# Second mixture: the scaled combine weights are turned by VectorE blocks and DMAs instead of TensorE transposes

## The chip, the cores and the metric

The kernel runs on one core of one Trainium2 chip. The metric is the device time of one execution in microseconds (us). Before the change three runs took 1120.14, 1126.13 and 1126.85 us, median 1126.13 us. The execution that the profiler recorded took 1125.19 us; its span from the first to the last instruction is 1123.3 us, so 1.9 us lie around the span.

## The reference

Three stages follow each other: an attention block, a first mixture of experts with slots, and a second mixture whose weights are balanced. Only the last is touched by the change:

```python
def _moe_ref(x, phi, w1, w2):            # the first mixture
    ...
    c = exp(logits - logits.max(1)); c /= c.sum(1) + 1e-9     # (2304, 32)
    return c @ slot_out                                       # slot_out: (32, 512)

def _moe2_ref(x, w_gate, w1, w2):        # the second, N, D, E, F = 2304, 512, 8, 1024
    logits = x @ w_gate
    P = exp(logits - logits.max())
    for _ in range(8):                   # balance rows and columns
        P /= P.sum(1) + 1e-9
        P /= P.sum(0) + 1e-9
        P *= N / E
    for e in range(E):
        h = maximum(x @ w1[e], 0)
        out += P[:, e:e+1] * (h @ w2[e])
```

Since x = c @ slot_out, the kernel never forms x in the second mixture. It takes x @ w1[e] as c @ (slot_out @ w1[e]). P is positive, so P[:, e] is multiplied into c ahead of the maximum, and the products of an expert can be added up without a further factor. All products are made to nearly full float32 precision from a rounded part ("high", h) and a remainder ("low", l).

## The kernel before

The 2304 tokens are 18 tiles of 128. A **unit** is two token tiles (256 tokens) of one expert; an expert has nine units (NU = 9), eight experts have 72, and they run one after the other. Each unit has seven **steps** k = 0 to 6.

`c4T` holds the combine weights with 128 partitions: four blocks of 32 slots (high, high, low, low), along the tokens. `a4s[e]` holds slot_out @ w1[e] in the matching blocks. `layer1(g)` (L1118) multiplies both: 8 matmuls per unit give the hidden values of the unit. `layer1(g + 1)` is issued behind step 1 of unit g.

From unit 5 on a unit's second layer is a seven-product scheme (Strassen's kind): `product` (L1424 to L1426) issues 12 matmuls of 128x256 per step, so 84 per unit, from sums of hidden values s1 to s4, a11, a12, a22 (high and low) and sums of weights T1 to T4, BB1, BB2. `hidden` makes the hidden sums on VectorE (DVE, L1142, L1155), ScalarE (ACT, L1138, L1148) and GpSimd (POOL, L1159); `collect` adds the products into accA, accB and accD on DVE (L1440).

Beside this, each expert e from 1 on needs, ahead of its own units:

- `load_w1`, `load_raw`: eight loads of 512 KB on the queue of SyncE (SP), L984 and L977.
- `prepare_a` (L1065): 32 small matmuls in unit 1 of expert e - 1 into the PSUM tile pa; `split_a` (L1074, L1076), and `move_a` (L1098): 16 DMAs of 32 KB into `a4s[e]`.
- the weight sums and their high and low parts: `w_sum`, `w_hi`, `w_lo` (L1018, L1021, L1027), mostly on POOL.
- its scaled combine weights in `c4T`. This is what the change replaces. Five times per expert (`c_steps`), for units 0-1, 2-3, 4-5, 6-7 and 8, in units 6, 7 and 8 of expert e - 1 and in units 0 and 1 of expert e itself: `scale_c` multiplies c by P on DVE (L1289), rounds on ACT (L1294), writes the high part twice on ACT (L1298) and the remainder twice on DVE (L1299); `turn_c` (L1304) transposes four tiles of 128x128 on TensorE (PE) into the PSUM tile pc, two tiles the fifth time; `store_c` (L1309) copies pc to `c4T` on ACT.

PE, DVE, ACT and POOL run in the order in which the program is written (a manual schedule): `beside(s, f)` puts a helper at step s = 7 * unit + k behind that step's product. Each engine works through its own list and waits at the first instruction whose inputs are not there. The SP queue issues its DMAs in the order that the planner gives it, one after the other. Each DMA uses one of eight semaphores in turn, so it waits for the one that was issued eight places earlier.

Of the kernel before, what the change touches and what calls it, by code (L numbers as in the profile page):

```python
# [8 lines left out]
F32 = mybir.dt.float32  # L9
BF16 = mybir.dt.bfloat16  # L10
F32R = mybir.dt.float32r
# [10 lines left out]
def infini_attention_soft_moe_sinkhorn_moe(  # L22
# [1002 lines left out]
    def w_lo(e, nm, i, g):  # L1025
# [9 lines left out]
    Cw = mD.tile([P, NTT, NS], F32, name="Cw")  # L1035
    sel = mD.tile([P, 4, 160], F32R, name="sel")
    nc.vector.tensor_scalar(
        out=sel.rearrange("p j c -> p (j c)"), in0=ones[:, 0:1].to_broadcast([P, 640]),
        scalar1=0.0, scalar2=None, op0=ALU.mult,
# [19 lines left out]
    def prepare_a(e):  # L1059

        w1 = w1s.pop(e)
        pa = aux("pa")
        for c in range(KD):
            for j in range(4):
                nc.tensor.matmul(  # L1065
                    pa[32 * j : 32 * j + 32, 0:256], soT[:, c, :], w1[j][:, c, :],
                    start=(c == 0), stop=(c == KD - 1),
                )
        a2s[e] = pa

# [126 lines left out]
    m2 = mS.tile([1, 1], F32, name="m2")  # L1197

    def gate_slots():
        soB = G["soB"] = mB.tile([P, KD, 4, NS], F32, tag="c4", name="soB")  # L1200
        nc.scalar.activation(out=soB, in_=soR.to_broadcast([P, KD, 4, NS]), func=AF.Copy)
# [84 lines left out]
    def scale_c(e, u0, u1):  # L1286
        T0, n = 2 * u0, 2 * (u1 - u0)
        cP = mB.tile([P, 4, NS], F32, tag="cP", name="cP")[:, 0:n]
        nc.vector.tensor_tensor(  # L1289
            out=cP, in0=Cw[:, T0 : T0 + n], in1=Pr[:, T0 : T0 + n, e : e + 1].to_broadcast([P, n, NS]),  # L1290
            op=ALU.mult,
        )
        chi = mB.tile([P, 4, NS], F32R, tag="chi", name="chi")[:, 0:n]
        nc.scalar.activation(out=chi, in_=cP, func=AF.Copy)  # L1294
        c4 = cs_[e, u0] = mB.tile([P, 4, 4, NS], F32, tag="c4", name="c4")
        hb = chi.bitcast(F32).rearrange("p t (o s) -> p t o s", o=1).to_broadcast([P, n, 2, NS])
        cb = cP.rearrange("p t (o s) -> p t o s", o=1).to_broadcast([P, n, 2, NS])
        nc.scalar.activation(out=c4[:, 0:n, 0:2, :], in_=hb, func=AF.Copy)  # L1298
        nc.vector.tensor_tensor(out=c4[:, 0:n, 2:4, :], in0=cb, in1=hb, op=ALU.subtract)  # L1299

    def turn_c(e, u0, u1):
        pc = G["pc"] = aux("pc")
        for t in range(2 * (u1 - u0)):
# [4 lines left out]
    def store_c(e, u0, u1):  # L1308
        nc.scalar.activation(  # L1309
            out=c4T[:, UT * u0 : UT * u1], in_=G["pc"][:, 0 : UT * (u1 - u0)], func=AF.Copy  # L1310
        )


    side = {}
# [27 lines left out]

    def c_steps(v, e, u0, u1):
        at(v, 1, scale_c, e, u0, u1)
        at(v, 2, turn_c, e, u0, u1)
        at(v, 3, store_c, e, u0, u1)

    for k, u0, u1 in ((-1, 5, 7), (2, 7, 9)):
        for n, f in enumerate((scale_c, turn_c, store_c)):
            at(RAW - 1, k + n, f, 0, u0, u1)  # L1350
    s = 1
    for i in range(2):
# [9 lines left out]
    for e in range(1, E):  # L1362
        v = NU * (e - 1)
        for i in range(5):
            c_steps(v + 6 + i, e, 2 * i, min(2 * i + 2, NU))
        at(v, 0, load_w1, e, e % 2)
# [3 lines left out]
        at(v + 1, 4 + (e == 1), split_a, e)  # L1370
        at(v + 1, 5 + (e == 1), move_a, e)
        for i in range(2):
# [41 lines left out]
    def product(g, k):  # L1414
# [7 lines left out]
        wh, wl = W[e, b, "h"], W[e, b, "l"]  # L1422
        for f in range(KH):
            nc.tensor.matmul(o_, hh[:, f, :], wh[:, f, :], start=f == 0, stop=False)  # L1424
            nc.tensor.matmul(o_, hh[:, f, :], wl[:, f, :], start=False, stop=False)  # L1425
            nc.tensor.matmul(o_, hl[:, f, :], wh[:, f, :], start=False, stop=f == KH - 1)  # L1426
        return o_
# [197 lines left out]
```

## Time and profile before

| | |
|---|---|
| median of three runs | 1126.13 us |
| the profiled execution | 1125.19 us, span 1123.3 us |
| granted TensorE clock, mean over the span | 0.988 |
| second mixture, seven-product units | about 387 us to the end |
| issues of `a` by `move_a` | 112 in all, 32 KB each |

The page's first part gives busy time by engine, its second part the same in 40 slices of 28 us each with the granted clock. A matmul's row lasts 0.28 us, but the next one starts 0.11 us later, since they are pipelined; so the distance between starts, not the length of a row, tells what a matmul costs. In the chain of waits "PE l L1118 x8" is a unit's `layer1`; from one such row to the next is exactly one unit's work on PE.

### The profile page before, as it was taken

To read this page: it belongs to the slowest core of one execution; us is meant where nothing else is said; L and a number is where in the kernel's file an instruction comes from. 1 tells how busy PE (TensorE), PEld (TensorE's weight loads), DVE (VectorE), ACT (ScalarE), POOL (GpSimd) and SP (SyncE) were. 2 spreads that over 40 slices of the span, in tenths; PEclk is the share of its full clock that TensorE was granted. 3 is DMA by queue.
4 is the path that set the end of the run, shared out by engine and by line. 5 is a ranking of instruction groups with operands and counts; after the bars stand their busy time and mean duration, and the time that the engine had idled before them with its cause. 6 is when DMAs were issued, how large, how long until landed. Compare 5 with 4: busy or idle time off the path is not lost.

```text
span 1123.3 us, 24568 instructions
## 1 busy us (share of the span) xinstructions
PE 1080.5 (96%) x9269; PEld 988.4 (88%) x9269; DVE 832.4 (74%) x1813; ACT 644.3 (57%) x1392; POOL 703.7 (63%) x634
## 2 busy tenths in 40 slices
PE   6999898988999999999999999999999999999998
PEld 4777777764477899999999999999999999999998
DVE  7777777764167467788778878877877787788876
ACT  7988888751242666456545645654564464556442
POOL 5755545410153587678678767867776786778665
PEclk9999999997989999999999999999999999999999
DMA  7677875348912003003200400220040022000111
GB/s 178 200 218 228 239 248 136 86 152 363 370 56 75 1 5 147 20 1 113 58 1 2 150 21 1 99 71 3 1 151 20 1 95 73 5 2 6 53 57 57
DMA packets 42647, 105.73 MB, mean 94 GB/s; under 512 B 8225, under 2 KB 18593, under 8 KB 38433
## 3 DMA queue, kind: packets, MB, share of 16 engines
q1 hardware_dynamic: 42096, 104.07, 28.5%
q8 instruction: 74, 1.21, 0.4%
q14 instruction: 45, 0.36, 0.1%
q10 hardware_dynamic: 432, 0.09, 0.0%
HBM read 95.74 MB, written 4.72 MB: 89 GB/s over the span
## 4 chain that ended last, share of the span: by engine, by line
PE 83%; DVE 5%; issue 4%; DMA 4%; ACT 3%; POOL 1%; SPq 0%; DVEq 0%; ACTq 0%; POOLq 0%
PE y L1424 19%; PE y L1425 19%; PE y L1426 19%; PE l L1118 6%; PE po L455 4%; PE pt L418 2%; PE y L1391 2%; DMA wm<-in_moe_w_dram 2%; PE pa L1065 1%; PE pc L1304 1%; PE ps L373 1%; ACT sm L379 1%; DMA w<-in_moe_w_dram 1%; PE ps L374 1%; PE ps L359 1%
## 5 line engine op out<-in xcount | busy, mean ns | idle before, releaser
L1142 DVE SCALAR_TENSOR_TENSOR f<-l,f 128x512 f32<-128x512 f32 x268 | 184.1, 687 | 61.2 <-ACT a11h L1148 53.6
L1159 POOL TENSOR_TENSOR s1l<-f,s1h 128x512 fp32r<-128x512 f32 x67 | 90.2, 1347 | 153.6 <-ACT s1h L1148 153.6
L1440 DVE TENSOR_TENSOR accA<-accA,y 128x512 f32<-128x512 f32 x125 | 85.5, 684 | 42.8 <-PE y L1426 42.3
L1148 ACT ACTIVATE a12h<-l 128x512 fp32r<-128x512 f32 x72 | 43.2, 601 | 97.1 <-PE y L1426 91.4
L1159 POOL TENSOR_TENSOR s4l<-f,s4h 128x512 fp32r<-128x512 f32 x67 | 87.4, 1304 | 15.7 <-PE y L1425 13.0
L1440 DVE TENSOR_TENSOR accB<-accB,y 128x512 f32<-128x512 f32 x125 | 85.6, 685 | 5.6
L1159 POOL TENSOR_TENSOR s3l<-f,s3h 128x512 fp32r<-128x512 f32 x67 | 87.2, 1301 | 0.0
L1159 POOL TENSOR_TENSOR s2l<-f,s2h 128x512 fp32r<-128x512 f32 x67 | 87.0, 1298 | 0.0
L1118 PE MATMUL l<-c4T,a 128*128 128x256 f32 x576 | 80.3, 283 | 2.3 <-DVE a22l L1155 2.3
L1138 ACT ACTIVATE f<-l 128x512 f32<-128x512 f32 x67 | 39.7, 592 | 74.3 <-PE l L1118 73.2
L1027 POOL TENSOR_TENSOR BB1l<-raw,BB1h 128x512 fp32r<-128x512 f32 x32 | 41.4, 1305 | 61.7 <-ACT BB1h L1021 61.7
L1424 PE MATMUL y<-T2h,s2h 128*128 128x256 f32 x268 | 77.5, 289 | 0.0
L1118 PEld LDWEIGHTS l<-c4T,a 128*128 128x128 f32 x576 | 73.2, 192 | 4.2 <-DVE a22l L1155 3.8
L1424 PE MATMUL y<-BB2h,a12h 128*128 128x256 f32 x268 | 74.9, 279 | 0.0
L1425 PE MATMUL y<-BB2l,s4h 128*128 128x256 f32 x268 | 74.7, 279 | 0.0
L1424 PE MATMUL y<-BB1h,s3h 128*128 128x256 f32 x268 | 74.6, 278 | 0.0
L1426 PE MATMUL y<-BB1h,s3l 128*128 128x256 f32 x268 | 74.5, 278 | 0.0
L1425 PE MATMUL y<-BB1l,s3h 128*128 128x256 f32 x268 | 74.5, 278 | 0.0
L379 ACT ACTIVATE sm<-sm,mn 128x128 f32<-128x128 f32 (+3 forms) x128 | 70.8, 554 | 6.5 <-DVE mn L375 6.2
L1425 PE MATMUL y<-T2l,s2h 128*128 128x256 f32 x268 | 74.5, 278 | 0.0
L1426 PE MATMUL y<-T2h,s2l 128*128 128x256 f32 x268 | 74.4, 278 | 0.0
L1424 PE MATMUL y<-BB2h,s4h 128*128 128x256 f32 x268 | 74.3, 277 | 0.0
(315 smaller groups left out, 4203.9 us busy)
## 6 DMA issues: line engine op xcount, KB each, us to landing
wm<-in_moe_w_dram SPq DMA_DIRECT2D x32, 1024.0 KB, 8.2
raw<-in_moe_w_dram SPq DMA_DIRECT2D x32, 512.0 KB, 4.1
w<-in_moe_w_dram SPq DMA_DIRECT2D x32, 512.0 KB, 4.3
qd<-in_q_dram SPq DMA_DIRECT2D x30, 288.0 KB, 4.4
kd<-in_k_dram SPq DMA_DIRECT2D x30, 288.0 KB, 4.6
qp<-in_q_dram SPq DMA_DIRECT2D x15, 288.0 KB, 3.8
vt<-in_v_dram SPq DMA_DIRECT2D x16, 256.0 KB, 2.8
out_dram<-accB SPq DMA_DIRECT2D x18, 128.0 KB, 1.8
```

Of the source, the lines that this page charges most:

```text
L379: nc.scalar.activation(out=sm[:, 0:n], in_=sm[:, 0:n], func=AF.Exp, scale=-1.0, bias=mnc, accum_out=X.sums[:, i, h : h + 1],)
L455: nc.tensor.matmul(po[64 * h : 64 * h + 64, c0:w], X.vt[:, j, h, :], rhs, start=(j == 0), stop=(j == n - 1),)
L1027: eng(g).tensor_tensor(out=w_tile(e, nm, "l")[:, h], in0=full(e, nm, i), in1=w_tile(e, nm, "h")[:, h].bitcast(F32), op=ALU.subtract,)
L1118: nc.tensor.matmul(ph[:, f, :], a4s[e][:, P * (KH * j + f) : P * (KH * j + f) + P], c4T[:, UT * u : UT * u + UT], start=True, stop=True,)
L1138: nc.scalar.activation(out=f_tile(g, nm), in_=ph(g, nm), func=AF.Relu)
L1142: nc.vector.scalar_tensor_tensor(out=f_tile(g, nm), in0=ph(g, src), scalar=0.0, in1=b, op0=ALU.max, op1=op)
L1148: nc.scalar.activation(out=h_tile(g, nm, "h"), in_=ph(g, nm) if a else FU[g, nm], func=AF.Relu if a else AF.Copy)
L1159: nc.gpsimd.tensor_tensor(out=lo, in0=FU[g, nm], in1=hi, op=ALU.subtract)
L1424: nc.tensor.matmul(o_, hh[:, f, :], wh[:, f, :], start=f == 0, stop=False)
L1425: nc.tensor.matmul(o_, hh[:, f, :], wl[:, f, :], start=False, stop=False)
L1426: nc.tensor.matmul(o_, hl[:, f, :], wh[:, f, :], start=False, stop=f == KH - 1)
L1440: nc.vector.tensor_tensor(out=acc, in0=acc, in1=y, op=ALU.add)
```

## The change

For experts 1 to 7, 16 of the 18 token tiles are turned without PE, in two rounds of eight tiles (r = 0: units 0 to 3, r = 1: units 4 to 7):

- `part_c` multiplies c by P on POOL (128x256), `round_c` rounds it on ACT, `rest_c` takes the remainder on POOL.
- `blocks_c` transposes 32x32 blocks with one DVE instruction of 128x256 for the high and one for the low part.
- `move_c` puts the blocks into place: 16 DMAs of 32 KB per round on the SP queue, each of 32 partitions by 8 runs of 128 bytes.

Round 0 stands in units 4 and 5 of expert e - 1 (one unit later for e = 1), round 1 in unit 1 of expert e, steps 0 to 4. The two tiles left over (unit 8) are still scaled by `scale_c` and transposed by PE, now straight ahead of the 32 matmuls of the next `prepare_a`, into the unused half of the same PSUM tile; `store_c` follows at step 5. `move_a` goes from unit 1 to unit 3. In unit 0 of an expert, the products with B and T3 weights issue the four matmuls that use a low weight part last. The tile `sel` is shared with the blocks, and small tiles are laid into shared ones.

```diff
     def prepare_a(e):
         w1 = w1s.pop(e)
-        pa = aux("pa")
+        pa = a2s[e] = aux("pa")
+        if e > 1:
+            turn_c(e - 1, NU - 1, NU)
...
     def turn_c(e, u0, u1):
-        pc = G["pc"] = aux("pc")
+        pc = G["pc"] = a2s[e + 1][:, 256:] if 0 < e < E - 1 else aux("pc")
...
+    NR = 8
+    WR = NR * NS
+    ct_ = {}
+
+    def part_c(e, r):
+        cw = ct_[e, r] = cw_tile()
+        nc.gpsimd.tensor_tensor(
+            out=cw[:, 0:WR].rearrange("p (t s) -> p t s", s=NS), in0=Cw[:, NR * r : NR * r + NR],
+            in1=Pr[:, NR * r : NR * r + NR, e : e + 1].to_broadcast([P, NR, NS]), op=ALU.mult,
+        )
+
+    def round_c(e, r):
+        cw = ct_[e, r]
+        nc.scalar.activation(
+            out=cw[:, WR : 2 * WR].bitcast(F32R), in_=cw[:, 0:WR], func=AF.Copy
+        )
+
+    def rest_c(e, r):
+        cw = ct_[e, r]
+        nc.gpsimd.tensor_tensor(
+            out=cw[:, 0:WR], in0=cw[:, 0:WR], in1=cw[:, WR : 2 * WR], op=ALU.subtract
+        )
+
+    def blocks_c(e, r, z):
+        if z == 0:
+            ct_[e, r, "t"] = mD.tile([P, 640], F32, tag="sel", name="ct")
+        cw = ct_[e, r]
+        nc.vector.transpose(
+            ct_[e, r, "t"][:, WR * z : WR * z + WR], cw[:, WR * (1 - z) : WR * (2 - z)]
+        )
+
+    def move_c(e, r, zs):
+        ct = ct_[e, r, "t"]
+        to = c4T[:, 0:N].bitcast(F32).rearrange("p (t j n) -> p t j n", j=4, n=32)
+        for z in zs:
+            for j in range(4):
+                nc.sync.dma_start(
+                    to[32 * z : 32 * z + 32, NR * r : NR * r + NR, j],
+                    ct[32 * j : 32 * j + 32, WR * (z // 2) : WR * (z // 2) + WR].rearrange(
+                        "p (t n) -> p t n", n=32
+                    ),
+                )
...
-    def c_steps(v, e, u0, u1):
-        at(v, 1, scale_c, e, u0, u1)
-        at(v, 2, turn_c, e, u0, u1)
-        at(v, 3, store_c, e, u0, u1)
+    def c_round(s, e, r):
+        for k, f, *a in (
+            (0, part_c), (1, round_c), (2, blocks_c, 0), (5, rest_c), (6, blocks_c, 1),
+        ):
+            beside(s + k, f, e, r, *a)
+        beside(s + 3, move_c, e, r, (0, 1))
+        beside(s + 7, move_c, e, r, (2, 3))
...
+    at(NU * (E - 1) + 1, 3, turn_c, E - 1, NU - 1, NU)
...
         v = NU * (e - 1)
-        for i in range(5):
-            c_steps(v + 6 + i, e, 2 * i, min(2 * i + 2, NU))
+        c_round(7 * (v + 4 + (e == 1)) + 2, e, 0)
+        for k, f, *a in (
+            (0, part_c), (1, round_c), (2, blocks_c, 0), (2, rest_c), (3, blocks_c, 1),
+            (3, move_c, (0, 1)), (4, move_c, (2, 3)),
+        ):
+            at(v + 10, k, f, e, 1, *a)
+        at(v + 10, 1, scale_c, e, NU - 1, NU)
+        at(v + 10, 5, store_c, e, NU - 1, NU)
...
-        at(v + 1, 5 + (e == 1), move_a, e)
+        at(v + 3, 3 * (e == 1), move_a, e)
...
+        terms = ((hh, wh), (hh, wl), (hl, wh))
+        seq = [(f, t) for f in range(KH) for t in terms]
+        if u == 0 and e and (b[0] == "B" or b == "T3"):
+            seq = [(f, t) for f in range(KH) for t in terms[::2]] + [(f, terms[1]) for f in range(KH)]
+        for n, (f, (a, b)) in enumerate(seq):
+            nc.tensor.matmul(o_, a[:, f, :], b[:, f, :], start=n == 0, stop=n == 3 * KH - 1)
```

Three places of the order show the move. First PE in unit 1 of expert 2, around the third and fourth step, before (y are the products' PSUM tiles, w the tiles of w1, c the scaled weights; the number is a buffer's):

```order
L1425 MATMUL y_7287<-BB1l,s3h 128x256
L1426 MATMUL y_7287<-BB1h,s3l 128x256
L1304 MATMUL pc<-ident,c_7284 128x128 x2
L1424 MATMUL y_7310<-T2h,s2h 128x256
L1425 MATMUL y_7310<-T2l,s2h 128x256
...
L1426 MATMUL y_7310<-T2h,s2l 128x256
L1065 MATMUL pa<-w_0_7079,soT 32x256
L1065 MATMUL pa<-w_1_7081,soT 32x256
```

and with the change:

```order
L1492 MATMUL y_7269<-T2l,s2h 128x256
L1492 MATMUL y_7269<-T2h,s2l 128x256
L1315 MATMUL pa<-ident,cf 128x128 x2
L1068 MATMUL pa<-w_0_7050,soT 32x256
L1068 MATMUL pa<-w_1_7052,soT 32x256
```

The two transposes that are left stand directly ahead of `prepare_a`; the four turns of four transposes, such as "L1304 ... x4" in each of the four units before, have no row any more. On PE there are 112 rows fewer in all.

Second, DVE in the same unit, before:

```order
L1440 TENSOR_TENSOR accB<-accB,y_7236 128x512
L1289 TENSOR_TENSOR cP<-Cw,Pr 128x64
L1299 TENSOR_TENSOR c_7284<-cP,chi 128x2x64
L1440 TENSOR_TENSOR accA<-accA,y_7256 128x512
L1142 SCALAR_TENSOR_TENSOR f<-l_7274,f 128x512 x2
L1440 TENSOR_TENSOR accD<-accD,y_7287 128x256
L1142 SCALAR_TENSOR_TENSOR f<-l_7269,f 128x512
```

and with the change:

```order
L1506 TENSOR_TENSOR accB<-accB,y_7194 128x512
L1300 TENSOR_TENSOR cf<-Cw,Pr 128x64
L1310 TENSOR_TENSOR cf<-cf 128x2x64
L1506 TENSOR_TENSOR accA<-accA,y_7216 128x512
L1144 SCALAR_TENSOR_TENSOR f<-l_7234,f 128x512
L1352 STREAM_TRANSPOSE ct<-cw 128x256
L1144 SCALAR_TENSOR_TENSOR f<-l_7234,f 128x512
L1506 TENSOR_TENSOR accD<-accD,y_7246 128x256
L1352 STREAM_TRANSPOSE ct<-cw 128x256
L1144 SCALAR_TENSOR_TENSOR f<-l_7229,f 128x512
```

The two block transposes of round 1 stand between the hidden sums of this unit. The second needs `rest_c`, which POOL makes.

Third, the SP queue from the raw loads for expert 2 to the first w1 load for expert 3, before:

```order
L977 DMA raw_5733<-in_moe_w_dram 128x1024
L977 DMA raw_5735<-in_moe_w_dram 128x1024
L977 DMA raw_5737<-in_moe_w_dram 128x1024
L977 DMA raw_5739<-in_moe_w_dram 128x1024
L1098 DMA a_5918<-ahi 32x256 x4
L1098 DMA a_5918<-alo 32x256 x4
L1098 DMA a_5918<-ahi 32x256 x4
L1098 DMA a_5918<-alo 32x256 x4
L984 DMA w_1_7081<-in_moe_w_dram 128x1024
```

and with the change:

```order
L977 DMA raw_5700<-in_moe_w_dram 128x1024
L977 DMA raw_5702<-in_moe_w_dram 128x1024
L977 DMA raw_5704<-in_moe_w_dram 128x1024
L977 DMA raw_5706<-in_moe_w_dram 128x1024
L1361 DMA c4T<-ct 32x8x32 x16
L1100 DMA a_5904<-ahi 32x256 x4
L1100 DMA a_5904<-alo 32x256 x4
L1100 DMA a_5904<-ahi 32x256 x4
L1100 DMA a_5904<-alo 32x256 x4
L1361 DMA c4T<-ct 32x8x32 x16
L984 DMA w_1_7052<-in_moe_w_dram 128x1024
```

Round 1 of expert 1 (16 DMAs) now stands behind the raw loads and ahead of `move_a`, and round 0 of expert 2 behind `move_a`, ahead of the next loads.

## Rows read from the trace of the kernel before

**Rows 1.** The page, first and second part: busy time by engine, then the granted clock in 40 slices.

```profile
PE 1080.5 (96%) x9269; PEld 988.4 (88%) x9269; DVE 832.4 (74%) x1813; ACT 644.3 (57%) x1392; POOL 703.7 (63%) x634
...
PEclk9999999997989999999999999999999999999999
```

**Rows 2.** Windows: two units without transposes and one with four.

```profile
core 0: us, PE busy (x) PEld busy (x) DVE busy (x) ACT busy (x) POOL busy (x), PEclk, DMA share, GB/s
655.14:665.57 10.43, 10.43 (x95) 10.43 (x94) 7.99 (x13) 5.17 (x9) 7.26 (x6) 1.00 0.10 24
952.30:963.14 10.84, 10.84 (x95) 10.84 (x94) 7.97 (x13) 5.11 (x9) 7.57 (x6) 1.00 0.10 23
498.84:510.03 11.19, 11.19 (x98) 11.19 (x98) 10.01 (x16) 6.10 (x12) 8.96 (x8) 1.00 0.01 2
```

**Rows 3.** Chain of waits in order of time: start us, us, what.

```profile
399.05 0.91 PE l L1118 x8
...
457.13 0.91 PE l L1118 x8
...
556.25 0.91 PE l L1118 x8
...
597.96 0.91 PE l L1118 x8
608.85 0.91 PE l L1118 x8
...
642.08 1.18 PE l L1118 x8
655.14 0.91 PE l L1118 x8
665.57 0.91 PE l L1118 x8
...
952.30 0.94 PE l L1118 x8
963.14 0.94 PE l L1118 x8
...
1050.74 0.91 PE l L1118 x8
```

**Rows 4.** Timeline of PE: start us, us, instruction; the distance of starts is the pitch.

```profile
500.60 0.28 PE L1424 MATMUL y<-BB1h,s3h 128*128 128x256 f32 x1
500.71 0.28 PE L1425 MATMUL y<-BB1l,s3h 128*128 128x256 f32 x1
...
734.95 0.28 PE L1424 MATMUL y<-BB2h,s4h 128*128 128x256 f32 x1
735.14 0.38 PE L1425 MATMUL y<-BB2l,s4h 128*128 128x256 f32 x1
```

**Rows 5.** DMA issues: KB each, median us to landing; then SP's timeline.

```profile
a<-ahi SPq DMA_DIRECT2D x56, 32.0 KB, 1.8
mbd<-in_M_prev_dram SPq DMA_DIRECT2D x8, 65.0 KB, 3.7
...
648.60 2.41 SPq L1098 DMA_DIRECT2D a<-ahi  x4
```

**Rows 6.** Groups by line and shape from 450 us on: busy us, mean ns of one, idle.

```profile
L1299 DVE TENSOR_TENSOR c<-cP,chi 128x256 f32<-128x256 f32 x24 | 20.9, 870 | 10.1 <-ACT chi L1294 10.1
L1440 DVE TENSOR_TENSOR accD<-accD,y 128x256 f32<-128x256 f32 x120 | 49.9, 415 | 2.9 <-PE y L1426 1.3
L1338 POOL TENSOR_TENSOR accD<-accD,accA 128x256 f32<-128x256 f32 x9 | 7.2, 797 | 4.9 <-DVE accA L1440 4.9
```

**Rows 7.** Timelines of POOL and DVE in unit 1 of expert 3.

```profile
640.45 1.29 POOL L1159 TENSOR_TENSOR s4l<-f,s4h 128x512 fp32r<-128x512 f32 x1
645.93 1.29 POOL L1159 TENSOR_TENSOR s1l<-f,s1h 128x512 fp32r<-128x512 f32 x1 [4.19 <-ACT s1h L1148]
...
644.50 1.49 DVE L1142 SCALAR_TENSOR_TENSOR f<-l,f 128x512 f32<-128x512 f32 x2 [0.50 <-ACT a11h L1148]
```

More of the change, by code (lines that the diff above doesn't have):

```diff
@@ L1035, in infini_attention_soft_moe_sinkhorn_moe @@
     Cw = mD.tile([P, NTT, NS], F32, name="Cw")
-    sel = mD.tile([P, 4, 160], F32R, name="sel")
+    sel0 = mD.tile([P, 640], F32, tag="sel", name="sel").bitcast(F32R)
+    sel = sel0.rearrange("p (j c) -> p j c", j=4)
     nc.vector.tensor_scalar(
-        out=sel.rearrange("p j c -> p (j c)"), in0=ones[:, 0:1].to_broadcast([P, 640]),
+        out=sel0, in0=ones[:, 0:1].to_broadcast([P, 640]),
         scalar1=0.0, scalar2=None, op0=ALU.mult,
@@ L1068, in prepare_a @@
                 )
-        a2s[e] = pa
     def split_a(e):
@@ L1197, in infini_attention_soft_moe_sinkhorn_moe, with cw_tile @@
     m2 = mS.tile([1, 1], F32, name="m2")
+    def cw_tile():
+        return mB.tile([P, 768], F32, tag="cw", name="cw")
     def gate_slots():
-        soB = G["soB"] = mB.tile([P, KD, 4, NS], F32, tag="c4", name="soB")
+        soB = G["soB"] = cw_tile()[:, 0:512].rearrange("p (c a s) -> p c a s", c=KD, a=4)
         nc.scalar.activation(out=soB, in_=soR.to_broadcast([P, KD, 4, NS]), func=AF.Copy)
@@ L1287, in scale_c @@
         T0, n = 2 * u0, 2 * (u1 - u0)
-        cP = mB.tile([P, 4, NS], F32, tag="cP", name="cP")[:, 0:n]
+        if e:
+            cw = mB.tile([P, 2, CW], F32, tag="ft", name="cf").rearrange("p a c -> p (a c)")
+        else:
+            cw = cw_tile()
+        o_ = 4 * NS * (2 if e else 4)
+        w = n * NS
+        cP = cw[:, o_ : o_ + w].rearrange("p (t s) -> p t s", s=NS)
         nc.vector.tensor_tensor(
@@ L1292, in scale_c @@
         )
[L1293 to L1296, printed above, removed]
+        chi = cw[:, o_ + w : o_ + 2 * w].rearrange("p (t s) -> p t s", s=NS)
+        nc.scalar.activation(out=chi.bitcast(F32R), in_=cP, func=AF.Copy)
+        c4 = cs_[e, u0] = cw[:, 0:o_].rearrange("p (t a s) -> p t a s", a=4, s=NS)
+        hb = chi.rearrange("p t (o s) -> p t o s", o=1).to_broadcast([P, n, 2, NS])
         cb = cP.rearrange("p t (o s) -> p t o s", o=1).to_broadcast([P, n, 2, NS])
@@ L1422, in product @@
         wh, wl = W[e, b, "h"], W[e, b, "l"]
[L1423 to L1426, printed above, removed]
+        terms = ((hh, wh), (hh, wl), (hl, wh))
[4 more added lines that the diff above has]
+            nc.tensor.matmul(o_, a[:, f, :], b[:, f, :], start=n == 0, stop=n == 3 * KH - 1)
         return o_
```

## The prediction

> **What bounds the kernel now.** I read the page first: PE is busy for 96% of the span, and from the sixteenth slice on the granted clock reads 9, the highest digit, in every slice [rows 1], and 1.00 in the windows of the second mixture [rows 2]: its upper level, 2.4 GHz. So the clock is no lever here. Next come the windows of the second mixture: in each unit PE is busy for the whole of it, DVE for 8.0 to 10.0 us, POOL for 7.3 to 9.0 us, ACT for 5 to 6 us [rows 2]. PE alone sets the end there. What an edit is worth is the PE time it takes out, plus the stalls of PE that it ends, less those that it makes. The chain of waits gives the currency: the distance between two `layer1` rows is one unit on PE. A unit without anything beside its 92 matmuls takes 10.43 us (655.14 to 665.57) [rows 3], or 0.113 us per matmul, the pitch that the timeline shows between two starts (500.60, 500.71) [rows 4].
>
> The same rows show something the busy shares hide. From 952.30 to 963.14 lies one unit with the same 92 matmuls, and it takes 10.84 us [rows 3], with PE just as full and the clock at 1.00 [rows 2]. Every matmul starts 0.118 us after the last, not 0.113. I call it the **slow pitch**. It persists from matmul to matmul; it lasted for four units here. It begins or ends only where the stream of products is interrupted: by transposes, by `prepare_a`, or by a stall. Such a stall is seen at 735.14, where a product waits for a low weight part, 0.19 us after the start before it in place of 0.11 [rows 4]. What starts it I can't say from the trace. So each interruption is a draw. By the pitch behind them, of the 28 four-transpose turns 6 were followed by it, as in the unit of 11.19 us [rows 2], and of the six `prepare_a` one, the one ahead of 952.30; a `layer1` row of 0.94 us in place of 0.91 marks it [rows 3].
>
> **The change, part by part.** *PE.* Seven experts lose four turns of four transposes, 112 in all. One such turn at the fast pitch makes a unit 10.89 us (597.96 to 608.85), so 0.46 us [rows 3], and 28 of them 12.9 us. But the turns also cost by what they leave behind, so I take whole experts. The unit that holds `prepare_a` and two transposes takes 13.06 us (642.08 to 655.14), of which 0.27 us is a wait in `layer1` (1.18 in place of 0.91) [rows 3]; so 12.79 us is what stays of it. An expert without other turns and at the fast pitch is then 8 x 10.43 + 12.79 = 96.23 us. Experts 2 to 6 ran from 457.13 to 952.30, five experts, 495.17 us; 5 x 96.23 is 481.15, so 14.0 us go. In expert 1, 399.05 to 457.13 is 58.08 us against 4 x 10.43 + 12.79 = 54.51: 3.6 us. The last expert, 952.30 to 1050.74, took 98.44 us; it has no `prepare_a`, and 8 x 10.43 + (10.43 + 0.23) = 94.10: 4.3 us. **Together 21.9 us**: 12.9 us of transposes, and 9.0 us of slow pitch and small stalls that come with them.
>
> *The slow pitch afterwards.* `prepare_a` remains, with the two transposes now in front of it, one interruption per expert, and 1 in 6 of these was followed by the slow pitch. With nothing behind it to end it, it would last the nine units to the next: 9 x 0.41 = 3.7 us. With a chance of 1 in 6 in each of seven experts, one such expert is the likeliest count (39%), none 28%, two 23%. I give back one: 3.7 us.
>
> *The DMAs.* 32 per expert come onto the SP queue, 224 in all. In the trace one DMA of `a` is issued every 0.6 us (four in 2.41 us), and lands after 1.8 us; mbd moves 64 partitions by 4 runs of 260 bytes, 256 runs as a move has, and lands after 3.7 us [rows 5]. A round of 16 thus takes 15 x 0.63 + 1.8 to 3.7, 11 to 13 us. Round 0 has over two units until `layer1` of the next expert. Round 1 is the tight one: the first block transpose stands behind the first hidden sum of unit 1, which starts at 644.50 in expert 3 [rows 7], so its DMAs start near 645.6; the first reader, `layer1` of unit 4, is two unit starts behind 642.08, at 665.57 [rows 3]. That leaves 20 us less the 0.27 us stall, 19.7 us, so 6 to 8 us of slack. I cost it at nothing; the cover is two units of products, and below is what it costs if it fails. `move_a`, pushed to unit 3 behind these, has until unit 8: nothing.
>
> *DVE.* Out go ten operations per expert, of which the 128x256 one alone takes 870 ns [rows 6]; in come four block transposes. The trace has no such operation. The nearest 128x256 rows give 415 ns (accD) and 870 ns (two inputs from SBUF) [rows 6]; a transpose has one input, as accD has one from SBUF, so I take 415. In unit 1 of an expert this is 8.0 us of the plain unit [rows 2] plus some 0.5 us for the two small operations plus 0.8 to 1.7 us: 10.2 us at the most, below 10.43, and near the 10.01 us that a four-turn unit already carried [rows 2]. Nothing.
>
> *POOL.* Four operations of 128x256 at 797 ns [rows 6], at most the 1.3 us of a 128x512 one [rows 7]. In unit 1 POOL is idle for 4.19 us ahead of s1l [rows 7], and both operations of round 1 go there. In units 4 and 5 one each, on 7.3 to 9.0 us [rows 2]. Nothing.
>
> *ACT* loses four copies of 128x512 and eight small activations per expert and gains two: nothing. *The reordered products* keep their twelve matmuls; they end stalls like that of 735.14, whose 0.08 us and slow pitch are in the 9.0 us already. Waiting for eight DMA semaphores is not new to `layer1`: unit 0 of each expert did so for `a`.
>
> **Sum**: 1125.2 - 21.9 + 3.7 = 1107.0 us. The profiled execution lies 0.9 us below the median of 1126.13, within the spread of the three runs.
>
> **Rivals.** *1. The slow pitch stays in most experts.* For it: in the last expert it held over four units [rows 3], and the turns that used to end it are gone. Against: five of six `prepare_a` ended it. Three to seven experts give 1103.3 + 3 x 3.7 to 7 x 3.7, 1114 to 1129 us, so no change. By the 1 in 6 alone it has 10%; as the new neighbour of `prepare_a` may change the draw for all, I say 15%.
>
> *2. Round 1 lands late, and the kernel is slower.* Place: `layer1` of unit 4 in seven experts. Each DMA waits for the one eight places earlier, so with a landing time L a round takes 15 x L / 8 + L once L is above 5 us. It is late from L = 6.9 us (2.88 x 6.9 = 19.7), takes the whole gain of 3.1 us per expert at L = 7.9 us, and at L = 10 us it is 9 us late, 63 us in all, 1170 us. For it: runs of 128 bytes in place of the 1024 of `a`, and no DMA of the trace moves so many. Against: the 3.7 us for as many runs of 260 bytes, out of HBM and with other loads in flight [rows 5]. 8%. The Trainium skill ("DMA: Bandwidth & Descriptors", Specifications) speaks for this rival: below 512 bytes a transfer is a read, a change and a write, and off line rate. If that doubled the 3.7 us to 7.4, the round would be 1.6 us late, and the sum 1118 us in place of 1107. By that rule mbd's 260-byte rows should pay it already; the trace has them at 3.7 us.
>
> *3. A new wait reaches PE.* DVE's second block transpose waits for POOL, which waits for ACT, which waits for POOL behind s4l; behind it on DVE stand s3 and the accumulations that free PSUM. By rows it is ready at 640.45 + 1.29 + 0.80 + 0.6 + 0.80 = 643.9, before DVE comes to it, and still with 1.3 us per POOL operation (644.9) [rows 7]. If 1 us per expert got through, 1114 us. 7%.
>
> **Chances.** Forecast with none to two experts at the slow pitch, 1103 to 1111 us: 70%. Rivals: 15, 8 and 7%. About 1%, 11 us, is what a measurement of this kernel can tell from no change. Faster by more (below 1115 us): all of the forecast, rival 3 mostly, a part of rival 1, 81%. Same: the rest of rivals 1 and 3 and the mild end of rival 2, 13%. Slower: rival 2 with L over 8.4 us, 6%. The range that leaves out 2 in 10 goes from 1101 (no slow pitch, and 2 us for the run) to 1116 us, with three experts at the slow pitch, or a new wait.
>
> **What would show it.** After: `layer1` rows 10.43 us apart in seven or eight units of each expert, and about 12.8 us where `prepare_a` stands. Slow pitch: 10.84 us in a row of units. Rival 2: `layer1` of unit 4 waiting for a DMA, and c4T landings of over 7 us. Rival 3: PE waiting for DVE in unit 1 or 5. The forecast is wrong if transposes that are gone leave units at 10.9 us, or the sum of the distances falls by less than 14 us.

## The result, and the profile after

The changed kernel took 1135.0 us in the median of 20 runs (1120.26 to 1142.43), the kernel before 1124.74 (1120.14 to 1131.56) beside it. The ratio is 1.0056, 95% interval 1.0037 to 1.0075: no faster, and if anything 0.6% slower. (The comparison leaves the longest runs out, so the ratio is nearer to 1 than the medians are; experiment e10 shows what one run of that length consists of.) The forecast was 1107.0 us.

The profiled run after took 1120.26 us, the shortest of the 20 and 14.7 us below their median; what is read from it holds for that run. First the page: busy time of PE and the granted clock, which answer to [rows 1], and the DMA issues (KB each, median us to landing), to [rows 5].

```profile
PE 1074.0 (96%) x9157; PEld 982.7 (88%) x9157; DVE 804.7 (72%) x1785; ACT 617.9 (55%) x1322; POOL 719.1 (64%) x662
...
PEclk9999999996999999999999999999999999999999
...
c4T<-ct SPq DMA_DIRECT2D x224, 32.0 KB, 2.0
```

The 112 transposes are gone (9269 instructions of PE to 9157), but PE's busy time fell by 6.5 us, not by the 12.9 that they cost. The new DMAs land after 2.0 us. Now groups by line from 380 us on: instruction, count, busy us, mean ns. They are the operations that [rows 6] were to stand in for.

```profile
L1352 DVE STREAM_TRANSPOSE ct<-cw 128x256 f32<-128x256 f32 x28 | 12.2, 436 | 3.0 <-POOL cw L1344 2.7
L1344 POOL TENSOR_TENSOR cw<-cw 128x256 f32<-128x256 f32 x14 | 10.4, 744 | 3.7 <-ACT cw L1338 3.7
L1331 POOL TENSOR_TENSOR cw<-Cw,Pr 128x256 f32<-128x256 f32 x14 | 9.1, 647 | 0.0
```

The chain of waits (start us, us, what) answers to [rows 3]; `layer1` is now L1120. The unit at 540.05, 636.92 and 736.86 is the one with `prepare_a`.

```profile
453.36 0.94 PE l L1120 x8
464.20 0.94 PE l L1120 x8
...
540.05 0.95 PE l L1120 x8
...
552.91 0.91 PE l L1120 x8
563.34 0.91 PE l L1120 x8
...
630.25 1.79 POOL BB2l L1027
...
636.92 1.19 PE l L1120 x8
...
650.17 0.94 PE l L1120 x8
...
736.86 0.97 PE l L1120 x8
...
749.74 0.91 PE l L1120 x8
...
946.58 0.91 PE l L1120 x8
...
1043.20 0.94 PE l L1120 x8
```

The units are what was forecast: 10.43 us at the fast pitch (552.91 to 563.34), 10.84 at the slow one (453.36 to 464.20), nothing at 10.9. But the pitch changes at every `prepare_a`: slow up to 540.05, then fast for one expert's length, then slow (650.17), and so on. Behind the last expert's two transposes, where no `prepare_a` stands, it is slow again (1043.20). And a POOL instruction, `BB2l`, stands on the path in unit 0 of the experts that run fast. The waits of PE's weight loads from 380 us on (us in all, times, longest) give its price:

```profile
PEld l L1120 <- DVE a22l L1157: 3.0, 5, 2.3
PEld y L1492 <- POOL BB2l L1027: 1.9, 4, 0.5
```

**Where the 13.3 us between 1107.0 and 1120.26 went**, against the 96.23 us of a fast expert. Three slow experts, 453.36 to 552.91 the first: 99.55, 99.57 and 99.57 us, 10.0 us over. Two fast ones, 552.91 to 650.17 the first, 97.26 us, 2.1 us over: 0.6 us each in unit 0, with the wait for POOL's `BB2l`, and 0.5 us each in the unit of `prepare_a` (636.92 to 650.17, 13.25 against 12.79), 0.28 of it the wait in `layer1` (1.19 in place of 0.91) that the forecast had taken off. The last one up to unit 65, 946.58 to 1043.20: 96.62 against 94.10, 2.5 us. Behind it five units at the slow pitch, 2.1 us, and the last 151 matmuls at 0.0045 us more each, 0.7 us. Together 17.4, less the 3.7 us that the forecast had given back: 13.7 us. Of the 0.4 us over, 0.2 are two further differences, the rest is rounding: `layer1` of 397.14 in this run came 1.9 us earlier than that of 399.05 before, and from there to 453.36 it took 56.2 us against the 54.51 of the forecast, 1.7 us more.

### The profile page after: what moved, and what is told of

It is laid out like the page before. It is cut to its first block, busy times and chain, and to the rows that moved or that the text cites. A ratio compares the mean times of both kernels' runs of the same rounds, so it can differ in the third digit from the quotient of the medians.

```text
span 1118.5 us, 24560 instructions
## 1 busy us (share of the span) xinstructions
PE 1074.0 (96%) x9157; PEld 982.7 (88%) x9157; DVE 804.7 (72%) x1785; ACT 617.9 (55%) x1322; POOL 719.1 (64%) x662
## 4 chain that ended last, share of the span: by engine, by line
PE 78%; issue 6%; POOL 5%; DVE 5%; ACT 3%; DMA 2%; SPq 0%; DVEq 0%; POOLq 0%; ACTq 0%
PE y L1492 55%; PE l L1120 5%; PE po L455 3%; PE pt L418 2%; POOL BB2l L1027 2%; PE ph L863 1%; DMA qp<-in_q_dram 1%; PE pso L885 1%; ACT sm L379 1%; PE pa L1068 1%; PE ps L373 1%; PE y L1455 1%; PE ps L374 1%; PE ps L359 1%; PE ps L354 1%
## 5 line engine op out<-in xcount | busy, mean ns | idle before, releaser
L1161 POOL TENSOR_TENSOR s1l<-f,s1h 128x512 fp32r<-128x512 f32 x67 | 87.1, 1300 | 128.7 <-ACT s1h L1150 116.6
L1120 PE MATMUL l<-c4T,a 128*128 128x256 f32 x576 | 79.2, 280 | 2.1 <-DVE a22l L1157 2.1
L1120 PEld LDWEIGHTS l<-c4T,a 128*128 128x128 f32 x576 | 72.3, 188 | 3.5 <-DVE a22l L1157 3.0
L1492 PE MATMUL y<-T2h,s2h 128*128 128x256 f32 x268 | 75.0, 280 | 0.0
L1492 PE MATMUL y<-T4h,a22h 128*128 128x256 f32 x268 | 74.7, 279 | 0.0
L1492 PE MATMUL y<-T4l,a22h 128*128 128x256 f32 x268 | 74.7, 279 | 0.0
L1492 PE MATMUL y<-T4h,a22l 128*128 128x256 f32 x268 | 74.7, 279 | 0.0
L1492 PE MATMUL y<-T1h,s1h 128*128 128x256 f32 x268 | 74.7, 279 | 0.0
L1492 PE MATMUL y<-T1l,s1h 128*128 128x256 f32 x268 | 74.7, 279 | 0.0
L1492 PE MATMUL y<-T1h,s1l 128*128 128x256 f32 x268 | 74.7, 279 | 0.0
```

Source lines behind the costliest of these rows:

```text
L1120: nc.tensor.matmul(ph[:, f, :], a4s[e][:, P * (KH * j + f) : P * (KH * j + f) + P], c4T[:, UT * u : UT * u + UT], start=True, stop=True,)
L1161: nc.gpsimd.tensor_tensor(out=lo, in0=FU[g, nm], in1=hi, op=ALU.subtract)
L1492: nc.tensor.matmul(o_, a[:, f, :], b[:, f, :], start=n == 0, stop=n == 3 * KH - 1)
```

## The experiments

Each experiment's runs stand beside runs of the kernel before on the same chip; ratios are to those. e1 to e4 share one such set, e5 to e8 a second, e9 to e11 a third, and e12 has a fourth, so times of different sets are compared by their ratios. Each profile is of one run.

**e1, the changed kernel again.** No edit.

> The changed kernel once more, for a second profile. Theory (the pitch of the products): the time follows the number of units that run at the slow pitch (10.84 us in place of 10.43), about 1105 us plus 0.41 us for each of up to 66 such units; a time of 1130 us or more shows the slow pitch in more than 50 units, and stalls of PE in the experts that sum to less than 5 us. Rival (late parts): the number of slow units stays near the 33 or so of the first profile, and what is longer is found in waits of PE for POOL, DVE or a DMA.

1124.8 us (1117.61 to 1128.74, 6 runs), ratio 0.9985 (0.9953 to 1.0016). The first three experts ran at the slow pitch, the rest fast, each from unit 2 on: another pattern than in the first profile, though every `prepare_a` again left the other pitch than the one it met. What it met was not fixed. In experts 2 and 3 the slow pitch ended in `layer1` of unit 1, where single starts came up to 0.03 us late, and `prepare_a` turned it to slow again; in expert 4 it lasted, and `prepare_a` turned it to fast. In experts 5 and 6 the wait in that `layer1` left the slow pitch, where the same wait had left the fast one in the first profile. The profiled run was the shortest, 1117.61 us, so what was expected of a run of 1130 us was not tested.

**e2, the two leftover transposes back in their old place**, at step 2, twelve matmuls ahead of `prepare_a`; all else as in the change.

```diff
-        pa = a2s[e] = aux("pa")
-        if e > 1:
-            turn_c(e - 1, NU - 1, NU)
+        if e < 2:
+            a2s[e] = aux("pa")
+        pa = a2s[e]
...
+    def turn_first(e):
+        a2s[e] = aux("pa")
+        turn_c(e - 1, NU - 1, NU)
...
+        if e > 1:
+            at(v + 1, 2, turn_first, e)
```

> The changed kernel with one difference: the two leftover transposes go back to step 2 of unit 1, twelve products ahead of prepare_a (their place in the kernel before), still into the same PSUM tile. Theory: in the kernel before, two transposes at that place left the slow pitch and prepare_a behind it ended it in five of six; directly ahead of prepare_a they no longer do, and prepare_a only changes the pitch into the other one. So here all experts from 2 to 6 run at the fast pitch, 96.3 us each, and the time falls to 1107 us (1103 to 1113). Rival (late parts; or the pitch is a draw): no change of the distances that depends on the place, 1120 to 1140 us as the changed kernel.

1114.33 us (1109.22 to 1119.67), ratio 0.9899 (0.9866 to 0.9932): 10.5 us below e1. This is above the 1103 to 1113 us that were expected. In its profile, of the run of 1111.05 us, all of experts 1 to 6 ran fast, at 97.0 to 97.1 us in place of the expected 96.3: unit 0 took 11.1 us, and the last expert's end was slow. The timeline of PE in unit 1 of expert 3 (start us, us, instruction) shows how:

```profile
635.43 0.28 PE L1498 MATMUL y<-BB1l,s3h 128*128 128x256 f32 x1
635.54 0.28 PE L1498 MATMUL y<-BB1h,s3l 128*128 128x256 f32 x1
635.66 0.38 PE L1319 MATMUL pa<-ident,cf 128*128 128x128 f32 x2
...
636.82 0.28 PE L1498 MATMUL y<-T2h,s2l 128*128 128x256 f32 x1
...
637.17 0.28 PE L1498 MATMUL y<-T2h,s2l 128*128 128x256 f32 x1
637.38 1.93 PE L1068 MATMUL pa<-w,soT 128*32 128x256 f32 x32
...
639.82 0.28 PE L1498 MATMUL y<-BB2l,a12h 128*128 128x256 f32 x1
...
640.16 0.28 PE L1498 MATMUL y<-BB2l,a12h 128*128 128x256 f32 x1
```

Ahead of the two transposes starts lie 0.11 us apart; behind them 0.35 us per three (636.82 to 637.17), the slow pitch; behind `prepare_a` 0.34 per three (639.82 to 640.16), the fast one. The transposes set the slow pitch for twelve matmuls, 0.05 us, and `prepare_a` turns it back. In the change they no longer do, so an expert that comes to `prepare_a` fast leaves it slow.

**e3, the kernel before with the transposes put in front of `prepare_a`**, and nothing else of the change.

```diff
-        pa = aux("pa")
+        pa = a2s[e] = aux("pa")
+        if e > 1:
+            turn_c(e - 1, NU - 1, NU)
...
```

> The kernel before with that one part of the change alone: the two leftover transposes directly ahead of prepare_a, in its PSUM tile; four turns of four transposes per expert stay. Theory: behind prepare_a the pitch is now the other one than ahead of it, so most experts, which come in fast, get the slow pitch for their four light units until the next turn of four ends it: light units of 10.84 us in at least half of the experts, 1.6 us each, 1126 to 1134 us. Rival: 1121 to 1127 us as before, light units at 10.43 us in five of six experts.

1125.85 us (1123.43 to 1129.15), ratio 1.0002 (0.9976 to 1.0029). Only the `prepare_a` of one expert left the slow pitch, for five units, until a four-transposes turn ended it. So the slow light units that were expected in at least half of the experts did not come, and that the turns cut a slow stretch short rests on this one case. The rule is not the whole of it either: here three of six `prepare_a` left the pitch other than they found it. In the three that did not, one matmul right behind came some 0.01 us late and the fast pitch followed; the same late matmul stands in two of the three others.

**e4, the change without the two transposes at all**: the calls of `turn_c` and of `store_c` for unit 8 are taken out, so the scaled weights of unit 8 stay those of expert 0.

> The changed kernel without the two leftover transposes and their copy (it leaves the scaled weights of unit 8 out for experts 1 to 7, so part of the output is another). It tells whether prepare_a alone changes the pitch. If it does: fast and slow experts alternate or the slow pitch stays for whole experts, as in the changed kernel, 1118 to 1140 us. If the two transposes in front are needed for it: all experts at the fast pitch, 1105 us (the forecast less 1.6 us of transposes). Rival (late parts): as the changed kernel less 1.6 us.

1126.76 us (1124.74 to 1134.79), ratio 1.0021 (0.9989 to 1.0052). It isn't the neighbourhood: `prepare_a` alone turns fast to slow, in the five experts of six that come to it fast, and slow to fast in the one that comes to it slow. Chain of waits, then the timeline of PE around the second of its rows:

```profile
530.41 0.94 PE l L1118 x8
541.25 0.93 PE l L1118 x8
554.03 0.94 PE l L1118 x8
...
540.62 0.28 PE L1488 MATMUL y<-BB1h,a11l 128*128 128x256 f32 x1
...
540.97 0.28 PE L1488 MATMUL y<-BB1h,a11l 128*128 128x256 f32 x1
541.09 1.09 PE L1118 MATMUL l<-c4T,a 128*128 128x256 f32 x8
542.02 0.28 PE L1488 MATMUL y<-BB1h,s3h 128*128 128x256 f32 x1
...
542.36 0.28 PE L1488 MATMUL y<-BB1h,s3h 128*128 128x256 f32 x1
```

Unit 0 is slow throughout, 10.84 us without a stall (530.41 to 541.25). In `layer1` of unit 1 the pitch turns: 0.35 us per three matmuls ahead of it (540.62 to 540.97), 0.34 behind it (542.02 to 542.36), with single starts in between at most 0.02 us late. `prepare_a` then turns fast to slow for the next units (554.03). So it went in experts 2 to 4. What turns the pitch in `layer1` stays open. The profiled run, 1134.79 us and the longest, showed a second loss: three units 0 of 14.1 to 14.6 us, in which PE started nothing for 2.3 to 2.8 us, waiting for DVE's one `BB2l`.

**e5, as e2, with round 1 of each expert begun in unit 6 of the expert ahead instead of unit 10**, which is unit 1 of the expert itself.

```diff
-        for k, f, *a in (
-            (0, part_c), (1, round_c), (2, blocks_c, 0), (2, rest_c), (3, blocks_c, 1),
-            (3, move_c, (0, 1)), (4, move_c, (2, 3)),
-        ):
-            at(v + 10, k, f, e, 1, *a)
+        c_round(7 * (v + 6) + 4 + 4 * (e == 1), e, 1)
```

> The kernel with the two transposes set apart from `prepare_a`, and with round 1 of each expert (`part_c`, `round_c`, `rest_c`, `blocks_c`, `move_c`) begun in unit 6 instead of unit 10, so that `part_c` no longer stands on POOL behind the last expert's `add_u`. Theory (the last expert's two stalls of 0.48 and 0.8 us are ACT waiting for that `part_c`): unit 65 has no stall over 0.2 us, 1.3 us less than the kernel it is built on, 1113 us in the median. The units 66 to 71 stay at 10.84 us, since two transposes without a `prepare_a` behind them stand there. Rival (round 1 is hidden in unit 10 and is not hidden in units 6 and 7, where POOL also makes the weights' sums): a new stall of 0.5 us or more in units 6 to 8 of each of seven experts, +3.5 us, 1117 us.

1113.26 us (1110.98 to 1116.22), ratio 0.9906 (0.9885 to 0.9926). The last expert's unit 1 (65 in the expectation, counted by its `layer1`) took 11.04 us with no stall over 0.2, against 12.26 in e2: as expected, and no new stall in units 6 to 8. The time by itself doesn't tell: the ratio is that of e2. The profiled run was the longest, 1116.22 us; in it one DVE `BB2l` took 5.10 us, in a unit 0 of 14.11 us, and one expert ran slow. There the two transposes, met at the slow pitch, left the fast one, and `prepare_a` turned that to slow; the same came once in e6 and once in e7.

**e6, as e5, with the second weights' high and low parts one step earlier.**

```diff
-        for nm, k in (("B11", 2), ("T3", 4), ("B21", 6), ("B22", 8)):
+        for nm, k in (("B11", 1), ("T3", 3), ("B21", 5), ("B22", 7)):
```

> The kernel of the early round 1, with the second weights' high and low parts (B11, T3, B21, B22) one step, 1.4 us, earlier in unit 8 of each expert. Theory (PE waits in unit 0 for POOL's last `BB2l`, 0.45 us, and behind it for `a22l`, 0.15 us, because POOL is behind its due time): unit 0 of each expert falls from 11.12 to about 10.45 us, seven times 0.65, 4.6 us less, 1108 us. Rival (where DVE's one `BB2l` falls among POOL's instructions decides: DVE is held until POOL pauses): some units 0 of 14 us, +3.7 us each, 1115 us or more.

1107.38 us (1106.29 to 1113.01), ratio 0.9863 (0.9841 to 0.9885): 5.9 us less, 4.6 expected. Unit 0 took 10.45 to 10.74 us where the expert ran fast.

**e7, as e6, with four transposes at the last expert's turn** (the same two done twice).

```diff
-        for t in range(2 * (u1 - u0)):
+        n = 2 * (u1 - u0)
+        for t in range(4 if e == E - 1 else n):
             nc.tensor.transpose(
-                pc[:, P * t : P * t + P], cs_[e, u0][:, t].rearrange("p a s -> p (a s)"), ident
+                pc[:, P * t : P * t + P], cs_[e, u0][:, t % n].rearrange("p a s -> p (a s)"), ident
```

> The kernel of the early weights, with four transposes instead of two at the last expert's turn (the two leftover ones done twice, the copies unused). Theory (four transposes leave the products at the fast pitch, two leave them at the slow one): units 66 to 70 take 10.43 us instead of 10.84, and the 151 matmuls from unit 71 on 0.113 us instead of 0.118: 5 x 0.41 + 0.75 - 0.11 = 2.7 us less, 1105 us. Rival (what leaves the slow pitch behind at the last expert is the stall at the turn, not the number of transposes): no change against the kernel of the early weights.

1103.96 us (1102.17 to 1107.69), ratio 0.9825 (0.9804 to 0.9845): 3.4 us below e6, 2.7 expected. Chain of waits of the last expert, from the turn at 1022.43 on, at the fast pitch; in e6 and e5 it was slow.

```profile
1022.43 0.91 PE l L1124 x8
1033.33 0.91 PE l L1124 x8
1043.75 0.91 PE l L1124 x8
```

**e8, as e4, without DVE's low part of B22** (that half keeps old values).

```diff
-                at(v + 8, k + i + (nm[0] == "B" and nm[1] == "2"), w_lo, e, nm, i, "D" if nm == "B22" and i else "P")
+                if nm != "B22" or i == 0:
+                    at(v + 8, k + i + (nm[0] == "B" and nm[1] == "2"), w_lo, e, nm, i, "P")
```

> The kernel without the two leftover transposes, and without DVE's low part of B22 (each expert's second half of that low part is left as it was). Theory (DVE's one subtraction of two SBUF tiles against POOL's: either POOL's third `BB2l` is drawn out from 1.30 to 1.75 us, or DVE is held until POOL pauses, 4.8 us, and PE waits 2.3 to 2.7 us for it and then runs at the lower clock): no unit 0 over 12 us in any expert, POOL's third `BB2l` 1.30 us in all of seven, the stall of 0.45 us at the third product gone; with all units at the slow pitch the highest run is at most 1128 us and no more than 5 us over the lowest. Rival (POOL is late by itself, and DVE's instruction only stands beside it): units 0 of 14 us stay, and runs up to 1135 us.

1114.9 us (1112.08 to 1119.93), ratio 0.9928 (0.9903 to 0.9953). No unit 0 was over 12 us. The rows of POOL's `BB2l` (min, median, max in ns), of the change and then of e8, show the contact from POOL's side:

```profile
L1027 POOL TENSOR_TENSOR BB2l<-raw,BB2h x21: 1298/1334/1784, 431.0 to 1023.9; 128x512 fp32r<-128x512 f32 x21
```

```profile
L1027 POOL TENSOR_TENSOR BB2l<-raw,BB2h x21: 1289/1302/1334, 431.4 to 1018.9; 128x512 fp32r<-128x512 f32 x21
```

Beside DVE's subtraction POOL's takes up to 1.78 us; without it never over 1.33. That is the 0.45 us by which PE waited in unit 0, which now took 10.7 us where the expert ran fast, against 11.2 in the first profile. Two parts of what was expected missed: not all units ran slow, since four of six `prepare_a` were now entered slow; and the runs spread over 7.9 us, not 5.

**e9, as e7, with the products in their old order**, high x low behind high x high for every f: the lines `if u == 0 and e ...` and `seq = ... terms[::2] ...` are taken out.

> The kernel with four transposes at the last turn, its first unit of each expert with the products in their old order (high x low right behind high x high, for every f). What the reordering was worth: in the old order the product of a weight needs its low part 10 matmuls, 1.1 us, sooner. Theory (the low parts of the shifted kernel still land within 0.2 us of the moment that the third and fourth products need them): 0.3 to 1.1 us more per expert in seven experts, 2 to 8 us, 1106 to 1112 us, and a wait of PE for `BB1l` or `BB2l` in unit 0 of every expert. Rival (the low parts have been there for over 1.1 us, and the new order is worth nothing): no change, 1104 us.

1103.28 us (1102.9 to 1106.66), ratio 0.979 (0.9765 to 0.9814), the best of all, and hardly apart from e7. The rival held: with the weights a step earlier, the reordering is worth nothing that these runs show. What it is worth at the weights' old place wasn't tried.

**e10 and e11, two more profiled runs of the changed kernel**, one run each.

> The changed kernel itself, once more with a profile, to see what a time above 1130 us consists of, if one comes. Theory (each expert at the slow pitch adds 3.7 us, each DVE `BB2l` held by POOL some 3 us): the time is the number of units at 10.84 us times 0.41, plus 3 us for each unit 0 above 13 us, on 1104 us, to within 3 us; the two kinds of `prepare_a`, entered at the fast pitch and left at the slow one, or the reverse, hold in all of six. Rival (the pitch behind `prepare_a` is a draw): entered and left at the same pitch in two or more of six.

> The changed kernel itself, a second look of the same kind, with the same two expectations.

1139.64 and 1125.07 us. e10 shows what one long run is. DVE's seven `BB2l` in the profile of the first run, and in e10 (x7: min, median, max ns):

```profile
L1027 DVE TENSOR_TENSOR BB2l<-raw,BB2h x7: 1057/1396/1490, 432.7 to 1023.1; 128x512 fp32r<-128x512 f32 x7
```

```profile
L1027 DVE TENSOR_TENSOR BB2l<-raw,BB2h x7: 1035/4791/5174, 433.8 to 1041.0; 128x512 fp32r<-128x512 f32 x7
...
  PEld y L1492: 12.0, 5
```

Five of the seven took about 5 us, and PE waited 12.0 us for them. One of them, in unit 0 of expert 3: DVE, POOL and PE in the timeline, and the window from 637.70 on (us, busy time by engine, granted clock, DMA share, GB/s).

```profile
634.29 5.17 DVE L1027 TENSOR_TENSOR BB2l<-raw,BB2h 128x512 fp32r<-128x512 f32 x1
...
632.64 3.83 POOL L1027 TENSOR_TENSOR BB2l<-raw,BB2h 128x512 fp32r<-128x512 f32 x3
636.38 1.31 POOL L1161 TENSOR_TENSOR s1l<-f,s1h 128x512 fp32r<-128x512 f32 x1
637.61 1.30 POOL L1161 TENSOR_TENSOR s2l<-f,s2h 128x512 fp32r<-128x512 f32 x1
640.89 1.29 POOL L1161 TENSOR_TENSOR s3l<-f,s3h 128x512 fp32r<-128x512 f32 x1 [1.98 <-ACT s3h L1150]
...
639.52 0.80 PE L1492 MATMUL y<-BB2l,s4h 128*128 128x256 f32 x2 [2.49 <-DVE BB2l L1027]
640.11 0.41 PE L1492 MATMUL y<-T4h,a22h 128*128 128x256 f32 x1
640.32 0.41 PE L1492 MATMUL y<-T4l,a22h 128*128 128x256 f32 x1
```

```profile
637.70:641.20 3.50, 1.68 (x8) 1.68 (x9) 3.50 (x5) 0.63 (x1) 1.52 (x2) 0.70 0.25 75
```

POOL ran five subtractions on end, none of them drawn out, up to 638.91; DVE's ended 0.55 us later, at 639.46. In the first profile the same instruction at the same place (629.39) took 1.49 us, and POOL's third `BB2l` 1.79 (630.25) instead. So in these profiles one of the two gave way: POOL for 0.45 us, or DVE until POOL paused. PE waits for DVE, then its starts lie 0.21 us apart (640.11, 640.32) and the granted clock of the stretch falls to 0.70, towards its lower level, 1.2 GHz: the whole unit took 14.72 us in place of 11.16. The five units together (14.67, 14.72, 13.75, 14.93, 13.72, against 10.84 where the expert was slow, 11.12 where fast) lost 17.0 us, of the 19.4 by which this run is longer than the first profile's; the rest is more units at the slow pitch. The sum that was expected falls 6 us short in both runs (e10: 1104, 34 slow units 13.9, five holds at 3 us, 1133; e11: 23 units and two holds, 1119): a hold costs 3.4 us, and 1104 us has none of the small stalls of unit 0 and of the last turn. `prepare_a` left the other pitch in all of six, in both.

The Trainium skill ("SBUF — State Buffer", section "SBUF: two separate sides") states that a DVE instruction with two SBUF inputs and a GpSimd instruction that reads SBUF lock each other out: the one that starts first has the shared port for its whole instruction. The trace agrees in part. POOL's third `BB2l`, begun behind DVE's subtraction, took 0.45 us longer, which would fit, though no run measures the lock itself. But the DVE instruction of 5.17 us stood while three POOL instructions started behind it (the third `BB2l`, s1l at 636.38 and s2l at 637.61) and ended before it; that a row of them may pass, the Trainium skill doesn't say there.

**e12, the change with only the weights a step earlier**, the transposes left in front of `prepare_a` (the one line of e6).

> The changed kernel with the second weights' high and low parts one step, 1.4 us, earlier in unit 8, and nothing else: the two transposes stay in front of `prepare_a`. Theory (two separate losses: `prepare_a` turns the pitch over, fast to slow and slow to fast; and DVE's `BB2l` is sometimes held by POOL's row of subtractions, which the shift ends): no unit 0 above 12 us; with the small stalls of unit 0 gone the pitch goes over in turns, so three of the six experts 2 to 7 run slow, 3 x 3.7 us, on the 1106.3 us of the best run of the kernel with both cures and its slow last expert, and 1.3 us for the last expert's two stalls: 1118.7 us, the runs within 1114 to 1124 us. Rival (the shift helped only together with the transposes set apart): units 0 of 13.7 to 14.9 us stay, and runs above 1128 us.

1116.47 us (1113.58 to 1127.02, 7 runs), ratio 0.9905 (0.9871 to 0.9939). Two separate losses, as expected: with the transposes still in front of `prepare_a` the pitch went over at all of six, and two whole experts (three were expected) and the last one's end ran slow. The part that said no unit 0 would be over 12 us missed: one took 14.72 us, with DVE's `BB2l` at 3.85 us; and two runs lie outside the 1114 to 1124 us. The shift doesn't end the hold, but it seems rarer: 1 in 28 such instructions in the profiles of e6, e7, e9 and e12, 11 in 49 in those of the change, e1, e2, e4, e5, e10 and e11. Holds come several to a run (five in e10), so this is one profile of four against four of seven.

## Why the prediction was wrong

**The transposes** (12.9 us): as costed. Units of 10.43 us at the fast pitch, none of 10.9 from 453 us on. **The DMAs, DVE, POOL**: landing in 2.0 us against 6.9 from which round 1 is late; block transposes 436 ns against the 415 taken; POOL's operations 647 and 744 ns against 797. Rival 2 did not come: runs of 128 bytes moved 32 KB in 2.0 us, about what `a` needs with its long runs [rows 5]. The rule of the Trainium skill that was weighed there ("DMA: Bandwidth & Descriptors", Specifications) doesn't show in these landings.

**The slow pitch afterwards** is the step that failed first. It read "1 in 6" as a draw at each `prepare_a`, and gave back one expert, 3.7 us; the profiled run has 12.8 us of it (three experts 10.0, the last one's end 2.8). In the kernels with the change it is no draw. In the twelve profiles of the change and of kernels made from it, all 72 `prepare_a` left the pitch other than the one they were entered at. In the kernel before all six were entered slow. The timeline of PE in unit 1 of expert 3 before shows why:

```profile
644.00 0.28 PE L1426 MATMUL y<-BB1h,s3l 128*128 128x256 f32 x1
...
644.34 0.28 PE L1426 MATMUL y<-BB1h,s3l 128*128 128x256 f32 x1
644.46 0.38 PE L1304 MATMUL pc<-ident,c 128*128 128x128 f32 x2
...
645.62 0.28 PE L1426 MATMUL y<-T2h,s2l 128*128 128x256 f32 x1
...
645.98 0.28 PE L1426 MATMUL y<-T2h,s2l 128*128 128x256 f32 x1
```

Three matmuls take 0.34 us ahead of the two transposes and 0.36 behind them, so they had made the pitch slow, and `prepare_a` turned it to fast in five of six; why the sixth stayed slow no run shows. The count of 1 in 6 held only for that state, and the change takes it away: it puts the transposes where they no longer set the pitch ahead of `prepare_a`, and what the small waits of unit 0 and `layer1` leave decides. What came is rival 1, three experts and the last one's end at the slow pitch. The forecast gave it 15%, for the case that the new neighbour of `prepare_a` changed the draw for all; it didn't look at the pitch just ahead of each `prepare_a`, which the timeline of PE shows. e2 puts the transposes back and gives 1114.33 us, 10.5 us below e1; e4 shows that it isn't the transposes' touch, but their absence ahead of it.

The second half of the same step, **nothing behind it to end it**, was right, and made the error nine units long each time. In e3, with the old turns behind it, the one slow stretch ended after five units.

**A new wait** (rival 3, 7%) is the second step that failed: *DVE* and *POOL* were both put at nothing, by their busy time. The wait came in another place than rival 3's, in unit 0, not unit 1. Its chain was sought on POOL's new operations; it was the old `BB2l` on DVE, beside POOL's. In the shortest run it is 1.2 of the 2.1 us of the two fast experts; in e10 it is 17.0 of the 19.4 us by which that run is longer. How much of the median of 1135.0 us it makes is not shown, since only the shortest of the 20 has a profile; nor why six runs of the same kernel in e1 had a median of 1124.8. "9.0 us of slow pitch and small stalls" that were to leave with the turns were therefore not all to be had: in unit 0 stalls of 0.5 us stay, and in four of the seven profiles with the weights at their old place one or more of some 3 us. What moved them is not settled. In the kernel before none of the seven `BB2l` on DVE took over 1.48 us in its profile; there DVE had the turn's own two operations ahead of it in unit 0, and its `BB2l` met POOL's third `BB2l` and s1l, one instruction later in POOL's row than after. That this shielded it wasn't tried by itself.

**The last expert** cost 2.5 us more than forecast up to unit 65. In e5 the early round 1 takes 1.2 us of it away: ACT stood in `round_c`, which waited 3.5 us for `part_c`, behind the last expert's `add_u` on POOL. That is rival 3's own chain, in its own unit, in one expert of seven. The prediction had placed round 1 beside unit 1 of a middle expert [rows 7], and not looked at the last one.

With both losses mended (e9) the time is 1103.28 us, 2.1% below the kernel before. That it is just the 1103.3 us that the sum gives without slow pitch is in part luck: the runs before beside it had a median of 1127.78 us, and the profile of e9 still has units 0 up to 0.3 us over 10.43 where the expert ran fast. But a gain of the size forecast was there, and these two losses, with the last expert's, took it back.

What stays open: what the two pitches are, why the order of interruptions turns one into the other, why three of six in e3 and one of six before did not, and what decides who gives way, POOL or DVE. At a distance of 0.80 us to the start of POOL's instruction DVE's was held in some experts and not in others.

## What to carry to other kernels

A frequency counted in the kernel before is a chance only if the change leaves alone what the counted events have in front of them: look up the state ahead of each event, not just behind it. Removing work that costs little by itself can remove what put an engine back into its better state, so ask of every edit which state it leaves to the long stretch behind it. Where two engines subtract SBUF tiles beside each other and PE needs the result within a microsecond, move that work earlier by a step before trimming anything else: it was worth 5.9 us here (e6 against e5).

## What the runs showed of the hardware that was not expected

- A stream of equal matmuls runs at either 0.113 or 0.118 us per start, at a granted clock of 1.00 in both, and stays so for nine units and more. 32 matmuls of `prepare_a` turned one into the other in 72 of 72 cases with the change, in five of six before and in three of six in e3. Two transposes twelve matmuls ahead of them, met at the fast pitch, left the slow one in all 17 cases of e2, e5, e6, e7 and e9; met at the slow pitch they left it in ten and the fast one in three. At the last turn four transposes left the fast pitch (e7, e9).
- A DVE subtraction of two SBUF tiles of 128x512 took 0.9 to 1.5 us beside POOL's and drew one of POOL's out from 1.30 to some 1.75 us, before the change too (s1l there), or was held for 3.8 to 5.2 us (12 of 77 cases).
- After PE had started nothing for 2.3 to 2.8 us, the starts came to lie 0.21 us apart for some 12 to 15 matmuls in three of the five units of e10 (granted clock 0.88 over the unit from 630.63 on), while in the other two the clock stayed at 1.00 (from 734.17 on).
